# The first transform of the first sequence with x as the loaded operand and its result kept on chip, and a new order of the work

## The chip, the core and the metric

The kernel runs on one core of a Trainium2 chip. TensorE multiplies matrices out of SBUF, the on-chip memory, into PSUM, its accumulation memory; VectorE and ScalarE work element by element and copy results out of PSUM; GpSimd fills a few constants; SyncE issues transfers (DMAs) between DRAM and SBUF. The metric is device time in microseconds (us), the median of several runs. Matmuls name a *loaded* (stationary) operand, whose columns become the rows of the result, and a *streamed* (moving) operand, whose columns become the columns of the result.

## What is computed

For each of 8 sequences of 3200 positions with 256 features:

```python
X = np.fft.rfft(x, axis=1)
Yr = Xr @ w_r - Xi @ w_i + b_r
Yi = Xr @ w_i + Xi @ w_r + b_i
Yr, Yi = shrink(Yr, 0.01), shrink(Yi, 0.01)   # sign(v) * max(|v| - 0.01, 0)
x = np.fft.irfft(Yr + 1j * Yi, n=3200, axis=1)
# then, on that x:
gate = sigmoid(sum over k of conv_w[k] * x delayed by 4 - k positions)
out = (gate * (x @ w_val)) @ w_out
```

All in float32; the moe weights come as 64-bit floats and are turned into 32 bits on chip.

## The kernel before

The transform of length 3200 is done in two steps, 3200 = 50 x 64. A position is n2 * 64 + n1.

1. *p1*, the first step over n2 (50 values): f1, a 50 x 50 matrix of cosines and sines in 64 columns, is the loaded operand and x the streamed one. Two halves h of n1 lie on partitions 0 to 49 and 64 to 113, and two column blocks go to the two halves of the output, so four matmuls of a quarter of the array (50x64) run side by side. The result s is copied to SBUF and stored in DRAM (`a_dram`), eight pieces u per sequence. Function `p1` does this for sequences 1 to 7, `p1_first` for sequence 0, whose x is loaded by SyncE's and ScalarE's queues together.
2. *p2*, 13 steps u of two frequencies t each (the last has one): a load brings the columns of t from `a_dram`, now with (part, n1) on 128 partitions; two fp32 matmuls with the columns as loaded operand and f2 as the streamed one give the spectrum s (line 590). ScalarE and VectorE split it into high and low fp32r parts and a sum of both parts; the products with the weights follow: k_ps (line 665, real plus imaginary with w_r) and y_ps (line 660). Bias, shrinking (lines 671 to 680), and after every second u the first inverse step z_ps (line 703, quarter tiles of 64x64 with g1, which for most t is f2 turned by a product with the identity, line 424). z goes to DRAM (`z_dram`).
3. *positions* and *gated*: z is loaded back (`zl`), the second inverse step y_p (line 759) fills `y_sb`, VectorE runs the taps (line 813), TensorE the two products v_ps and o_ps (line 791, in the last blocks 787), and SyncE stores `out`.

The order of all instructions is worked out when the program is built. Every piece of work is given to `plan.add` with its engine, its due time `at`, its expected length in ns, the pieces it depends on, and the buffer slots it opens. `Plan.order` plays the pieces through: it takes, for each engine, among the pieces that could start first, the one with the smallest due time; a bonus keeps pieces on part tiles (mode `q`) together. Due times are a step number plus an offset from the table `O` (lines 230 to 253). Expected lengths that the prediction uses are those of p1 (890), s2i (950), mix (1404), mix_sum (702) and s1i (1776).

At the start, TensorE has `warm` products on zeros between the four `p1_first` groups (lines 911 to 915). Many loads of constants wait until all 16 stores of sequence 0 have landed (`STORED`), the second part of f2 among them (lines 411 and 922); the weight splits wait until the last p1 group is copied (`START`).

The kernel writes sequence 0's columns and reads them back with these two lines, at the end of `p1_first` and in `p2`:

```python
engines[h][1].dma_start(out=dst[h, :, us[k] * 4 * D:(us[k] + 1) * 4 * D], in_=tl[ks[h]][k * HP:k * HP + N2, :])
nc.sync.dma_start(out=at_[:, 0:n, :], in_=src[:, ts[0]:ts[-1] + 1, :])
```

Of the kernel before, what the change touches and what calls it, by code (L numbers as in the profile page):

```python
# [10 lines left out]
F32 = mybir.dt.float32  # L11
# [21 lines left out]
def dft_constants():  # L33
# [37 lines left out]

    f1b = np.zeros((N2, HP))
    f1b[:, 0:N2] = f1.reshape(N2, N2)
    f2 = f2.reshape(NT, P, 2, N1).transpose(1, 0, 2, 3)
    f2 = np.concatenate([f2[:, :-1].reshape(P, NT // 2, 2, 2, N1).swapaxes(2, 3).reshape(P, -1), f2[:, -1].reshape(P, P)], axis=1)
    out = {"f1": f1b, "f2": f2, "g1": g1[-1].reshape(P, P), "g2": g2.reshape(N2, N2), "eye": np.eye(P)}
# [3 lines left out]
class Plan:  # L80
# [11 lines left out]
    def add(self, at, engine, busy, fn, uses=(), sets=(), new=None, delay=None, mode="r", kb=0, chain=None, extra=0):  # L92
# [10 lines left out]
        p = dict(n=n, at=at, engine=engine, busy=busy, fn=fn, before=before, new=new or {}, mode=mode, kb=kb, extra=extra,  # L103
# [7 lines left out]
    def order(self):  # L111
# [25 lines left out]
        mode, wire = "r", 0.0  # L137
        done = []

# [11 lines left out]
        while len(done) < len(pieces):  # L151
            best = None
            for e in engines:
                could = []
                for p in waiting[e]:
                    at = opens(p)
                    if at is not None:
                        could.append((max(free[e], p["ready"], at, wire - BACKLOG if p["kb"] else 0.0), p))
# [15 lines left out]
            if e == "PE":  # L174
# [3 lines left out]
                busy, delay, mode = busy + to, delay + to, p["mode"]  # L178
            if p["kb"]:
                wire = max(wire, start + 800) + p["kb"] * 1024 / WIRE  # L180
                delay = wire - start + 1400 + p["extra"]
            free[e] = start + busy
# [29 lines left out]
SWITCH = {"rq": 97, "fq": 97, "qr": 100, "qf": 100}  # L212
WEIGHTS = 130
CLOCK = ((40000, 1.6), (45000, 1.15))
WIRE = 230
BACKLOG = 5000
# [6 lines left out]
def act(n, kind="copy"):  # L223
# [7 lines left out]
     'together': 2.272,  # L231
     'later': 4.406,
     'load_x': -3.369,
     'p1': 1.752,
     'p1_step': 1.14,
     'load_a': -3.927,
     's2': -1.558,
     's1i': 1.333,
     'p3': 3.595,
     'load_z': -3.135,  # L240
     'y': 0.522,
     'conv': 1.176,
     'val': 2.74,
     'gate': -3.751,
     'project': 5.91,
     'late_val': 7.079,
     'late_out': 15.503,
     'turn': 0.967,
     'mix_sum': -0.635,
     'p1_1': -0.586,  # L250
     'load_x_1': -0.349,
     'p1_2': -1.603,
     'p3_0': 0.549}
WARM = 2, 1, 1, 1, 10
SLOTS = {"x": 3, "zl": 3, "y_hl": 2, "s1": 2, "a": 3, "xs": 2, "sx": 2, "xz": 1, "yb": 2, "tp": 3, "zst": 2,
# [7 lines left out]
def fourier_filter_then_gated_conv(ctx: ExitStack, tc: tile.TileContext, x, w_r, w_i, b_r, b_i,  # L263
# [5 lines left out]
    dram = ctx.enter_context(tc.tile_pool(name="dram", bufs=2, space=bass.MemoryType.DRAM))  # L269
    LATE_VAL, LATE_OUT = set(LATE[int(O["late_val"]):]), set(LATE[int(O["late_out"]):])  # L270
# [9 lines left out]
    b_sb = const.tile([P, 2 * D + 2 * P], F32, name="b_sb")  # L280
# [704 lines left out]
```

## Time and profile before

| | |
|---|---|
| median of 3 runs | 901.65 us (900.0 to 903.2) |
| profiled execution, span from first to last instruction | 897.1 us |
| TensorE matmul busy | 865.2 us (96%), 10370 records |
| TensorE weight load busy | 741.1 us (83%) |
| VectorE busy | 763.5 us (85%) |
| ScalarE busy | 603.7 us (67%) |
| DMA | 162.26 MB, 181 GB/s on the mean |
| share of the chain that ended last | PE 83%, DVE 10%, DMA 4%, ACT 2% |

The page gives, for one execution, the busy time of each engine and its share in 40 slices (digits are tenths). PE is TensorE, PEld its weight loads, DVE VectorE, ACT ScalarE, POOL GpSimd, SP SyncE; a q behind the name is the engine's instruction queue. A row of a group reads: line, engine, operation, result<-operands, tile of the array where it is a matmul, shape and count | busy us, mean ns of one | idle time of the engine just before and what ended it. An fp32 matmul leaves two records. Rows of the chain read: start, length, what. The profiled execution's own device time is not listed beside its span.

### The profile page before, as it was taken

To read this page: it belongs to the slowest core of one execution; us is meant where nothing else is said; L and a number is where in the kernel's file an instruction comes from. 1 tells how busy PE (TensorE), PEld (TensorE's weight loads), DVE (VectorE), ACT (ScalarE), POOL (GpSimd) and SP (SyncE) were. 2 spreads that over 40 slices of the span, in tenths; PEclk is the share of its full clock that TensorE was granted. 3 is DMA by queue.
4 is the path that set the end of the run, shared out by engine and by line. 5 is a ranking of instruction groups with operands and counts; after the bars stand their busy time and mean duration, and the time that the engine had idled before them with its cause. 6 is when DMAs were issued, how large, how long until landed. Compare 5 with 4: busy or idle time off the path is not lost.

```text
span 897.1 us, 24381 instructions
## 1 busy us (share of the span) xinstructions
PE 865.2 (96%) x10370; PEld 741.1 (83%) x10370; DVE 763.5 (85%) x1139; ACT 603.7 (67%) x924; POOL 4.4 (0%) x11
## 2 busy tenths in 40 slices
PE   7799979999999999999999999999999999999898
PEld 2478758898888988899888988989788899998675
DVE  1267787999899997999789996999969998999896
ACT  1256656877677867777677876877757776875654
POOL 0000000000000000000000000000001000000000
PEclk8889999999999999999999999999999999999999
DMA  6577777635755476555674566645674453513522
GB/s 203 198 233 239 228 227 217 210 130 182 236 180 179 159 229 218 190 183 160 217 235 158 163 204 217 222 131 174 215 223 154 139 172 109 178 62 116 180 75 91
DMA packets 103439, 162.26 MB, mean 181 GB/s; under 512 B 9154, under 2 KB 77636, under 8 KB 103332
## 3 DMA queue, kind: packets, MB, share of 16 engines
q1 hardware_dynamic: 102372, 157.44, 54.8%
q10 hardware_dynamic: 960, 3.28, 1.1%
q8 instruction: 81, 1.33, 0.6%
q14 instruction: 26, 0.21, 0.1%
HBM read 82.04 MB, written 78.64 MB: 179 GB/s over the span
## 4 chain that ended last, share of the span: by engine, by line
PE 83%; DVE 10%; DMA 4%; ACT 2%; issue 1%; ACTq 1%; SPq 0%
PE y_ps L660 14%; PE o_ps L791 13%; PE v_ps L791 12%; PE s L590 10%; PE z_ps L703 9%; PE k_ps L665 8%; PE y_p L759 7%; PE p L543 6%; DVE acc L813 4%; DMA x<-in_x 1%; PE v_ps L787 1%; DVE acc L855 1%; DVE gated L317 1%; DMA f_sb<-in_f 1%; DMA a_dram<-s 1%
## 5 line engine op out<-in xcount | busy, mean ns | idle before, releaser
L813 DVE SCALAR_TENSOR_TENSOR acc<-y_sb,cw_sb,acc 128x800 f32<-128x800 f32 (+1 forms) x264 | 255.9, 1018 | 17.6 <-ACT acc L810 17.2
L660 PE MATMUL y_ps<-w_sb,xs 128*128 128x256 f32 x1152 | 155.4, 284 | 0.6 <-DVE xs L648 0.6
L791 PE MATMUL o_ps<-gated,wo_sb 128*128 128x400 f32 x756 | 155.2, 351 | 0.6 <-DVE acc L855 0.6
L660 PEld LDWEIGHTS y_ps<-w_sb,xs 128*128 128x128 f32 x1152 | 144.5, 189 | 11.3 <-DVE xs L652 3.2
L791 PEld LDWEIGHTS o_ps<-gated,wo_sb 128*128 128x128 f32 x756 | 133.5, 188 | 3.1 <-DVE acc L855 0.8
L791 PE MATMUL v_ps<-y_hl,wv_sb 128*128 128x400 f32 x660 | 131.3, 346 | 0.5 <-ACT o L879 0.5
L590 PE MATMUL s<-f_sb,a 128*128 128x128 f32 x800 | 113.2, 284 | 8.2 <-ACT wo_sb L315 3.4
L791 PEld LDWEIGHTS v_ps<-y_hl,wv_sb 128*128 128x128 f32 x660 | 118.5, 188 | 1.6 <-ACT o L879 0.9
L590 PEld LDWEIGHTS s<-f_sb,a 128*128 128x128 f32 x800 | 101.7, 196 | 20.8 <-issue 6.9
L678 ACT ACTIVATE tp<-yb,nlam 128x512 f32<-128x512 f32 (+1 forms) x104 | 73.7, 708 | 38.7 <-DVE yb L674 38.6
L665 PEld LDWEIGHTS k_ps<-w_sb,xs 128*128 128x128 f32 x576 | 77.2, 190 | 20.8 <-issue 10.5
L703 PE MATMUL z_ps<-tp,g_sb 64*64 64x256 f32 x1536 | 93.4, 381 | 0.0
L665 PE MATMUL k_ps<-w_sb,xs 128*128 128x256 f32 x576 | 91.1, 294 | 1.2 <-DVE yb L671 0.9
L759 PEld LDWEIGHTS y_p<-g_sb,zl 50*64 50x64 f32 x4096 | 68.3, 135 | 18.1 <-issue 7.3
L315 ACT CAST gated<-acc 128x800 fp32r<-128x800 f32 x63 | 54.3, 862 | 38.2 <-DVE acc L855 38.0
L759 PE MATMUL y_p<-g_sb,zl 50*64 50x50 f32 x4096 | 72.5, 219 | 7.1 <-issue 4.2
L680 DVE SCALAR_TENSOR_TENSOR tp<-yb,tp 128x512 f32<-128x512 f32 (+1 forms) x104 | 70.0, 673 | 10.6 <-ACT tp L678 10.5
L671 DVE TENSOR_TENSOR yb<-k_ps,bias_sb 128x512 f32<-128x512 f32 x96 | 65.6, 684 | 15.7 <-PE k_ps L665 15.6
L703 PEld LDWEIGHTS z_ps<-tp,g_sb 64*64 64x64 f32 x1536 | 55.3, 133 | 27.4 <-issue 5.1
L855 DVE TENSOR_TENSOR acc<-v_ps,acc 128x800 f32<-128x800 f32 x64 | 62.9, 984 | 16.1 <-PE v_ps L791 12.7
L674 DVE TENSOR_TENSOR yb<-y_ps,yb 128x512 f32<-128x512 f32 x96 | 65.5, 683 | 7.4 <-PE y_ps L660 6.9
L714 ACT COPY z_t<-z_ps 128x1024 f32<-128x1024 f32 x48 | 48.5, 1010 | 25.7 <-PE z_ps L703 25.1
(80 smaller groups left out, 1016.7 us busy)
## 6 DMA issues: line engine op xcount, KB each, us to landing
zl<-z_dram SPq DMA_DIRECT2D x128, 200.0 KB
out<-o SPq DMA_DIRECT2D x63, 400.0 KB
a<-a_dram SPq DMA_DIRECT2D x96, 256.0 KB
z_dram<-z_t SPq DMA_DIRECT2D x48, 512.0 KB
x<-in_x SPq DMA_DIRECT2D x120, 200.0 KB
a_dram<-s SPq DMA_DIRECT2D x120, 200.0 KB
x<-in_x ACTq DMA_DIRECT2D x8, 200.0 KB
a_dram<-s ACTq DMA_DIRECT2D x8, 200.0 KB
```

The source lines that it names most:

```text
L590: nc.tensor.matmul(spec()[:, c, :, i, :], tl[ka][:, i, c * P:(c + 1) * P], f2_of(i), start=True, stop=True)
L660: nc.tensor.matmul(p[:, 1 - r, :], xm(hx, c, r), w_sb[:, m, hw, c, :], start=k == 0, stop=k == 5)
L665: nc.tensor.matmul(p, sm(hx, c), w_sb[:, 0, hw, c, :], start=k == 0, stop=k == 5)
L671: nc.vector.tensor_tensor(out=buffer(kb, "yb", [P, 2, D]), in0=tl[kk].rearrange("p (a d) -> p a d", a=1).to_broadcast([P, 2, D]), in1=bias ...
L674: add(at + 0.2, "DVE", dve(2 * D), lambda: nc.vector.tensor_tensor(out=yb(), in0=tl[ky], in1=yb(), op=ALU.add), [ky + (0,)], [kb + (0,)])
L678: nc.scalar.activation(out=buffer(kt, "tp", [P, 2, D])[:, 0:n], in_=tl[kb][:, 0:n], func=AF.Relu, bias=nlam)
L680: add(at + 0.2, "DVE", dve(n * D), lambda: nc.vector.scalar_tensor_tensor(out=tl[kt][:, 0:n], in0=tl[kb][:, 0:n], scalar=LAM, in1=tl[kt][: ...
L703: nc.tensor.matmul(p[e * HP:(e + 1) * HP, i, j * D:(j + 1) * D], g[i * HP:(i + 1) * HP, r, e * HP:(e + 1) * HP], tl[kts[j]][i * HP:(i + 1) ...
L759: nc.tensor.matmul(pv[h][e * HP:(e + 1) * HP, c, m, :], zt[half(h), m, c * P + e * HP:c * P + (e + 1) * HP], g2_sb[half(h), :], start=True ...
L791: nc.tensor.matmul(p[:, e, 0:TB], w[:, hw, c, e * P:(e + 1) * P], src(hy, c), start=n == 0, stop=n == 5)
L813: nc.vector.scalar_tensor_tensor(out=acc(c), in0=y_of(c, j), scalar=cw_sb[:, c, j:j + 1], in1=acc(c), op0=ALU.mult, op1=ALU.add)
L855: add(at + O["gate"], "DVE", dve(2 * TB), lambda: nc.vector.tensor_tensor(out=gate(), in0=hn(tl[kv][:, :, 0:TB]), in1=gate(), op=ALU.mult) ...
```

## The change

Sequence 0's first transform. x is loaded in 16 pieces: half r of the features goes to the partition half r, so that each partition holds one n2; 52 rows are read where 50 are used. Each piece is sorted by two copies into `x0`, with n1 inside a feature group. `p1_first` then takes 128 columns of `x0` (two groups of 64 positions n1 for one feature each) as loaded operand and the 50 columns of f1 as streamed one: 64 matmuls per half r, in four groups of 20, 20, 16 and 8. Each group is copied out of PSUM by two copies on ScalarE and two on VectorE, straight to where p2 reads its columns: `a0`, which lies in the memory of `y_sb`. p2 of sequence 0 thus has no load, and nothing of sequence 0 goes through `a_dram`.

The other parts: x of sequences 1 to 7 is loaded with the positions n1 in another order (1 KB pieces), and the rows of f2 and of the identity are permuted to match. Loads of x and z and stores of a move 52 rows instead of 50 (the last x keeps 50), and rows of `a_dram` have a pitch padded by 256 words. The columns of two steps u are loaded at once, by two DMAs, into two slots instead of three. z_ps uses 64x128 tiles, eight matmuls instead of 16 per group; the last z is copied twice. x0 shares its memory with the later y_hl and g_hl; b_sb is gone, its rows go into a zst buffer. f2 comes in parts of 2, 2, 4 and 5 steps, and the first two no longer wait for stores. The zeros ahead of y are filled after z of sequence 0 is stored. The warm-up is 32 products of 64 columns, then 3, 1 and 1 of 256. The bias product is due ahead of the p1 groups, p1 of sequence 1 after step 3 of sequence 0.

The planner gets a model of how instructions are fetched, of eight DMAs in flight and of the cold clock (`CLOCK`, `LANES`, `AHEAD`), new expected transfer sizes, and due times of their own for sequences 0, 1, 6 and 7 in `O`.

```diff
+    def p1_loads():
+        queue = (("SP", nc.sync), ("ACT", nc.scalar))
+        src = x.rearrange("b (n j u) (r c) -> u r (b n) j c", u=NB, j=2 * MB, r=2)
...
+        def load(u, r, q):
+            if r == 0:
+                room(("x", (0, u)), tags[u], 4 * D)
+            dst = tl["x", (0, u)][r * HP:r * HP + NF, :]
+            q.dma_start(out=dst.rearrange("p (j c) -> p j c", j=2 * MB), in_=src[u, r, 0:NF])
+
+        def sort(u, r, h, eng):
+            src = tl["x", (0, u)][half(r), h * 512:(h + 1) * 512].rearrange("p (j q g) -> p q j g", j=MB, q=2)
+            lo = h * NM + MB * u
+            dst = x0[half(r)].rearrange("p (q n g) -> p q n g", q=2, n=N1)[:, :, lo:lo + MB, :]
+            (nc.scalar.copy if eng == "ACT" else nc.vector.tensor_copy)(out=dst, in_=src)
...
+    def p1_first(r, i, at):
+        lo, hi = GROUPS[i]
+        kp = ("p1", (0, r, i))
+        cols = x0[half(r)].rearrange("p (k g) -> p g k", g=64)
+        nb = min(2, (hi - lo) // 4)
+        per = (hi - lo) // nb
         def products():
+            p = two_banks(kp)
+            for g in range(lo, hi):
+                k, s = (g - lo) // per, (g - lo) % per
+                nc.tensor.matmul(p[:, k, s * N2:(s + 1) * N2], cols[:, g], f1_sb[half(r), 0:N2], start=True, stop=True)
+
+        def keep(q, e, eng):
+            src = tl[kp][q * HP:(q + 1) * HP, 0:nb, 0:per * N2].rearrange("p b (g t e) -> p e b g t", g=per, e=2)[:, e]
+            c = r * P + q * 64
+            dst = a0[e * HP:(e + 1) * HP, :, c + lo:c + hi].rearrange("p t (b g) -> p b g t", b=nb)
+            (nc.scalar.copy if eng == "ACT" else nc.vector.tensor_copy)(out=dst, in_=src)
+        n = (hi - lo) * NT
+        add(at, "PE", 110 * (hi - lo), products, [...], [kp + (0,), ("turn", "p1", r, i)], {kp: "ps_2"},
+            mode="q", ins=4 * (hi - lo))
...
         def load():
-            at_ = buffer(ka, "a", [P, 2, D])
-            nc.sync.dma_start(out=at_[:, 0:n, :], in_=src[:, ts[0]:ts[-1] + 1, :])
+            at_ = buffer(ka, "a", [P, 4, D])
+            nt = n if last else 4
+            for e in range(2):
+                src = tl["a_dram", b][4 * u + e:4 * u + 2 * nt:2, 0:NH * NM * D]
+                nc.sync.dma_start(out=at_[e * HP:(e + 1) * HP, 0:nt, :], in_=src.rearrange("t (r c) -> r t c", c=D))
...
+        a_of = lambda i, c: tl[ka][:, odd + i, c * P:(c + 1) * P] if b else a0[:, ts[i], c * P:(c + 1) * P]
...
-                        for e in range(2):
-                            nc.tensor.matmul(p[e * HP:(e + 1) * HP, i, j * D:(j + 1) * D],
-                                             g[i * HP:(i + 1) * HP, r, e * HP:(e + 1) * HP],
-                                             tl[kts[j]][i * HP:(i + 1) * HP, r, :], start=r == 0, stop=r == 1)
+                        nc.tensor.matmul(p[:, i, j * D:(j + 1) * D], g[i * HP:(i + 1) * HP, r, :],
+                                         tl[kts[j]][i * HP:(i + 1) * HP, r, :], start=r == 0, stop=r == 1)
```

More of the change, by code (lines that the diff above doesn't have):

```diff
@@ L90, in __init__, with add @@
         self.opened, self.last = {}, {}
-    def add(self, at, engine, busy, fn, uses=(), sets=(), new=None, delay=None, mode="r", kb=0, chain=None, extra=0):
+    def add(self, at, engine, busy, fn, uses=(), sets=(), new=None, delay=None, mode="r", kb=0, chain=None, extra=0, moves=1, ins=0):
         n = len(self.pieces)
@@ L137, in order, with supplied @@
         mode, wire = "r", 0.0
+        landings = [0.0] * LANES
+        ran, fetched = 0, []
         done = []
+        def supplied(p):
+            m = -(-(ran + p["ins"] - AHEAD) // PACKET)
+            return fetched[m - 1] - p["busy"] * max(0, AHEAD + PACKET * (m - 1) - ran) / p["ins"] if m > 0 and p["ins"] else 0.0
         def opens(p):
@@ L178, in order @@
                 busy, delay, mode = busy + to, delay + to, p["mode"]
+                while PACKET * len(fetched) + TRIGGER <= ran + p["ins"]:
+                    fetched.append(start + p["busy"] * (PACKET * len(fetched) + TRIGGER - ran) / p["ins"] + FETCH)
+                ran += p["ins"]
             if p["kb"]:
@@ new lines, in p1_first @@
+    def p1_first(r, i, at):
[4 more added lines that the diff above has]
+        per = (hi - lo) // nb
+        def products():
+            p = two_banks(kp)
[8 more added lines that the diff above has]
+        n = (hi - lo) * NT
+        add(at, "PE", 110 * (hi - lo), products, [("x0", r, u, h) for u in range(8) for h in range(NH)] + [("f1", 0, 0)], [kp + (0,), ("turn", "p1", r, i)], {kp: "ps_2"},
+            mode="q", ins=4 * (hi - lo))
+        for j in range(4):
+            q, e_ = j // 2, j % 2
+            eng = "DVE" if q != e_ else "ACT"
+            add(at + 0.01 + 0.001 * j, eng, act(n) if eng == "ACT" else dve(n), lambda q=q, e_=e_, eng=eng: keep(q, e_, eng), [kp + (0,)],
+                [("a0", r, i, j)])
@@ L688, in p2 @@
         kts = [("tp", (b, v)) for v in both]
-        gs = [("g1", 2 * v, 0) for v in both]
-        nz = 1 if last else 4
+        gs = [g1_key(v) for v in both]
+        nz = 2 if last else 4
         def s1i():
@@ L743, in load @@
             for h in range(NH):
-                nc.sync.dma_start(out=zt[half(h)], in_=src[h, :, k * MB:(k + 1) * MB, :])
-        add(at + O["load_z"], "SP", 700, load, [("z_dram", b, u) for u in range(NU)], [kz + (0,)], {kz: "zl"}, kb=400, chain="zl")
+                nc.sync.dma_start(out=zt[h * HP:h * HP + NF], in_=src[h, :, k * MB:(k + 1) * MB, :])
+        add(at + off("load_z", b), "SP", 700, load, [("z_dram", b, u) for u in range(NU)], [kz + (0,)], {kz: "zl"}, kb=320, chain="zl", moves=2)
         def views():
@@ L950, in fourier_filter_then_gated_conv @@
                 later_constants(u)
+        if b == 0:
+            add(NU - 0.5, "POOL", 300, lambda: nc.gpsimd.memset(y_sb[:, :, 0, 0:H0 * N2], 0.0),
+                [("z_dram", 0, u) for u in range(NU)], [("y", -1, j) for j in range(3)])
         start = (b + 1) * T + O["p3"] + O.get(f"p3_{b}", 0.0)
```

337 lines of the change are left out of this document (185 added, 152 removed).

## The prediction

> **What bounds the kernel now.** I read the page first: busy shares, then the slices.
>
> ```profile
> span 897.1 us, 24381 instructions
> PE 865.2 (96%) x10370; PEld 741.1 (83%) x10370; DVE 763.5 (85%) x1139; ACT 603.7 (67%) x924; POOL 4.4 (0%) x11
> PE   7799979999999999999999999999999999999898
> DVE  1267787999899997999789996999969998999896
> PEclk8889999999999999999999999999999999999999
> ```
>
> TensorE is busy for 96% of the span, and the slices that fall short are the first two or three and a few at the end. A mean cannot tell what the start costs, so I cut the span into windows (columns: length, then busy time and count for PE, weight load, VectorE, ScalarE and GpSimd, then granted clock, DMA share, GB/s).
>
> ```profile
> 0.00:10.00 10.00, 6.07 (x14) 2.10 (x17) 0.48 (x1) 1.28 (x1) 1.14 (x9) 0.93 0.53 161
> 10.00:20.00 10.00, 9.60 (x46) 2.53 (x39) 2.45 (x2) 2.02 (x2) 0.00 (x0) 0.73 0.76 243
> 30.00:40.00 10.00, 8.01 (x22) 3.53 (x20) 2.12 (x4) 1.16 (x3) 0.00 (x0) 1.00 0.45 160
> 40.00:50.00 10.00, 8.35 (x42) 5.72 (x40) 2.32 (x5) 3.20 (x8) 0.00 (x0) 0.66 0.80 208
> 50.00:60.00 10.00, 10.00 (x87) 8.57 (x80) 7.19 (x14) 6.07 (x12) 0.00 (x0) 1.00 0.83 227
> 100.00:200.00 100.00, 94.55 (x1267) 79.91 (x1266) 89.80 (x166) 68.69 (x111) 0.00 (x0) 0.98 0.64 204
> 800.00:897.00 97.00, 87.82 (x924) 70.20 (x923) 83.26 (x106) 56.82 (x77) 0.00 (x0) 0.99 0.33 111
> ```
>
> From 50 us on, TensorE has no idle time for a long while. Before 50 us it looks busy too, but with 14 to 46 instructions in ten microseconds against 87, and much of that is warm-up filling. Two other stretches leave TensorE idle: 100 to 200 (100 - 94.55 = 5.45 us) and the last 97 us (9.2 us). What the start waits for is told by the chain that ended last:
>
> ```profile
> 29.74 6.81 DMA a_dram<-s
> 36.64 0.39 SPq L574
> 38.41 7.31 DMA f_sb<-in_f
> 45.85 2.05 PE s L590 x8
> 47.90 2.67 PE p L543 x16
> 50.57 0.90 PE k_ps L665 x6
> 51.47 1.40 PE y_ps L660 x12
> ```
>
> The reader should see three things. The last store of the first transform to DRAM takes until 36.6 us. Only then are the columns read back, and a part of the constants f2, held back behind the same stores, lands at 45.7. The first weight product (k_ps) runs at 50.57, and from there the kernel is bound by TensorE. So what the start loses is the time up to 50.57, less the useful work done in it.
>
> **The change, part by part.** *The first transform of sequence 0.* Removed: 64 matmul records of the old products, eight copies of 1024 columns, 16 stores and 13 loads of a, and the wait between them. Added: 16 loads of x by halves of the features, 32 sorting copies into x0, 128 fp32 matmuls of 50 columns with x as the loaded operand, and 32 copies out of PSUM into a0. I follow them in time.
>
> ```profile
> 2.00:4.00 2.00, 2.00 (x3) 0.67 (x2) 0.00 (x0) 0.00 (x0) 0.00 (x0) 1.00 0.60 187
> 42.00:44.00 2.00, 2.00 (x9) 1.37 (x7) 0.00 (x0) 0.96 (x2) 0.00 (x0) 0.66 0.95 230
> x<-in_x ACTq DMA_DIRECT2D x8, 200.0 KB
> ```
>
> Loads: 16 of 52 x 4096 bytes are 3.41 MB, the size of today's. Today's 50-row loads hold the share at 0.60, ten engines of sixteen, 187 / (0.60 x 16) = 19.5 GB/s each. In 42 to 44, with many 1 KB pieces, it is 230 / (0.95 x 16) = 15.1 each. The new pieces are of 512 bytes. I estimate 13 engines for 52 rows, since 10 divides 50 as 13 divides 52; that gives 253 or 197 GB/s and 13.5 or 17.3 us. From a first issue at 1.6 us, with about 1 us to land, the first half is there at 9.4 to 11.3 us and the second at 16 to 20. I take 10.3 and 18.
>
> ```profile
> L671 DVE TENSOR_TENSOR yb<-k_ps,bias_sb 128x512 f32<-128x512 f32 x96 | 65.6, 684 | 15.7 <-PE k_ps L665 15.6
> L647 DVE TENSOR_TENSOR sx<-s,sx 128x256 f32<-128x256 f32 x96 | 39.9, 415 | 24.5 <-ACT xs L644 22.6 <-PE s L590 1.7
> L615 DVE CAST xz<-xs 128x512 fp32r<-128x512 f32 x8 | 3.4, 419 | 0.0
> L453 ACT COPY bias_sb<-bias 128x512 f32<-128x512 f32 x1 | 0.6, 585 | 10.9 <-PE bias L449 10.9
> L317 DVE TENSOR_TENSOR w_sb<-st,w_sb 128x512 fp32r<-128x512 f32 x4 | 2.5, 685 | 0.0
> L341 DVE SCALAR_TENSOR_TENSOR st<-st 128x512 f32<-128x512 f32 x2 | 1.3, 682 | 0.0
> L449 PE MATMUL bias<-b_sb 1*128 1x256 f32 x8 | 2.0, 387 | 0.0
> L451 PE MATMUL bias<-b_sb 1*128 1x256 f32 x4 | 1.2, 408 | 0.0
> ```
>
> Copies: a sort of 512 elements is 0.42 us on VectorE (18 of them, 7.6 us) and 0.585 on ScalarE (14, 8.2 us). The copies out of PSUM have 500, 500, 400 and 200 elements by group, two on each engine, twice over: at 0.68, 0.68, 0.57 and 0.41 on VectorE 4 x 2.34 = 9.4 us. With the weight splits and sums (2.5 and 1.3 us) VectorE has 21 us to do between 4 and 31 us: it fits, without much room. ScalarE has less. So the copies hide behind loads and matmuls, except the last sort (0.59), the last two copies (0.8) and about 1 us by which I let the weight splits push VectorE. If that cover is gone, it is a rival below.
>
> ```profile
> 62.41 0.86 PE p L543 x8
> 66.90 0.89 PE s L590 x8
> 59.82 0.70 PE k_ps L665 x6
> 71.30 1.02 PE p L543 x8
> 60.52 1.89 PE z_ps L703 x32
> 72.31 1.73 PE z_ps L703 x32
> 74.04 0.90 PE k_ps L665 x6
> 788.20 0.92 PE y_p L759 x64
> 120.15 0.43 PE z_ps L695 x2
> ```
>
> Matmuls: no row has a 128-column load in front of a 50-column stream. Lower end: eight records of 128 columns take 0.89 us, so 0.111 each, and two records of 50 columns 2 x 0.043 = 0.087 us. Upper end: a pair never costs more than with 128 columns, 2 x 0.111 = 0.222. I take 0.110, the planner's figure in the diff, because its neighbours agree with the rows (890 against 0.86 us for p, 1404 against 1.40, 702 against 0.70, 950 against 0.92). Half the features are 64 matmuls, 7.0 us. The cold clock (0.73 in 10 to 20 us today) I put at 2.0 us once. First half: 10.3 + 0.6 + 7.0 + 2.0 = 19.9. The second half's x is sorted by 18.6, so TensorE goes on: 26.9. With the last copies 27.7, s2 to 28.6, and the steps up to the sorted sums on ScalarE and VectorE (0.37 + 0.42 + 0.41 + 0.41, and 0.5 between them) put the first k_ps at 30.7 instead of 50.57: 19.9 us earlier. The bias product (2.0 + 1.2 us, today just before 43 us) now stands ahead of the products, where TensorE waits for x. Constants: w_r, w_i, eye and the first 256 KB of f2 follow x on the queue, about 0.85 MB or 4 us after 18, so they land near 22, before 27.7.
>
> Taken back: two p1 of sequence 1 ran before 50.57 and now run later, 2 x 1.02 = 2.0 us; 1 us for VectorE as said. **Start: 19.9 - 2.0 - 1.0 = 17 us gained**, with 0.222 per matmul 14.3 less, with 0.087 up to 3 more. Sequence 1's x loads and stores, moved past the start on SP's queue, have from 22 us until their columns are wanted after thirteen steps, some 60 us; no sequence-0 column traffic competes with them.
>
> *The inverse first step (z_ps).* Eight matmuls of 64x128 replace 16 of 64x64. One full-array matmul of 256 columns takes 0.43; eight of them two at a time give 1.72, and today's group takes 1.73. So nothing is gained in streaming, and half the instructions go. What may be lost is at the boundary. Today z after p takes 1.73, z after another kind 1.89; p after z takes 0.86, p after another kind 1.02. A change between whole and quarter tiles thus costs 0.16, and none is paid between z and p or y_p. Following the chain I find 46 of the 48 groups of z, 15 with p or y_p ahead and 38 with one behind: 53 free boundaries. If half tiles next to quarter tiles pay like whole ones, that is 53 x 0.16 = 8.5 us; if not, nothing. Neither end is nearer, so I take 4.
>
> [...]
>
> *52 instead of 50 rows, padded pitch, a loads in pairs of steps.* All these DMAs run while TensorE is at 10.00 of 10.00, so they are worth nothing in the sum; without that cover it would be 0.2 us for each 200 KB transfer (10 engines against 13 at 19.5 GB/s, 1.05 against 0.83 us). z_t's last copy grows from 256 to 512 elements (some 0.2 us x 8 on ScalarE, 67% busy): nothing.
>
> *The order laid out anew.* TensorE's idle time after 50 us is what an order can win back.
>
> ```profile
> PE s L590 <- ACT wo_sb L315: 3.4, 1, 3.4
> ```
>
> The 5.45 us of 100 to 200 hold one stall of 3.4 us behind the conversion of w_out; the conversion stays, in the same steps. The last 97 us have 9.2. Bounds: 14.6 us won, or about as much lost by worse placing, say 6. I take 2 us won, close to none, since the diff changes none of the work there.
>
> **Sum**: -17 + 4 - 2 = -15 us, span 897.1 - 15 = 882.1. The median of the runs stands 901.65 - 897.1 = 4.55 above this span, so **886.6 us**; its own range is 881 to 890.
>
> **The rivals.** *Every boundary is paid*: +8.5 instead of +4, 891. For: the 0.16 is in the rows wherever tile sizes differ. Against: p to y_p, both with 64-row halves, pays nothing.
>
> *The weight load sets the pace of the new products* (0.222 instead of 0.110): 128 x 0.112 = 14.3 us later, and 886.6 + 14.3 = 901, or 897 without boundaries; call it 900. For: y_p has 64 loads in 0.92 us over four tiles, 57 ns per pair in a tile with a stream of 50 columns that takes 43, so there the load may already bind; twice the columns in a single tile would be 115 per pair. The operand is also read with a step of 64 words. [...]
>
> [...]
>
> *The copies bind instead of DRAM*: if the copies that move between partition halves with steps cost double, VectorE has 2 x 17 + 3.9 = 38 us from 4 us on, and k_ps comes at 44 or so: 13 us of the 17 go, 900. Then the change does not do what it says.
>
> *The order closes the gaps*: most of 14.6 us won, say 9, and no boundary paid: 897.1 - 17 - 9 + 4.55 = 876. For: idle TensorE stands in the windows. Against: the last stretch is bound by VectorE (83.26 of 97 busy).
>
> *Slower: the two half tiles take turns.* Place: z_ps, 48 groups. If tiles with all 128 columns do not run at once, a group costs 8 x 0.43 = 3.44, 48 x 1.71 = 82 us more: 901.65 - 19 + 82 = 965. It decides from 19 / 48 = 0.40 us more per group, that is from 2.13 us. For: no row shows two half tiles at work. Against: quarter tiles run four at once (16 matmuls in 1.73).
>
> **How the numbers follow.** About 0.3%, 2.7 us, is what a measurement of this kernel can tell from none: faster means below 898.9, slower above 904.4. Chances: forecast 0.40, every boundary paid 0.18, load-bound 0.14, copies 0.06, gaps closed 0.16, half tiles in turn 0.06. The two cases at 900 (0.20) split as 0.09 faster, 0.07 same, 0.04 slower. Faster 0.40 + 0.18 + 0.16 + 0.09 = 0.83, same 0.07, slower 0.06 + 0.04 = 0.10. The range runs from 873, a little under the gaps' case, to 900, which leaves out the turns, about half of the cases at 900 and a little below: some 0.18.
>
> **What would show it.** First k_ps near 31 us, no a_dram store before it, and the new products at 0.11 per matmul with 1 us or less between groups; at 0.2 the load binds. VectorE below 9 tenths from 10 to 27 us, else the copies bind. z_ps near 1.73 after p or y_p if boundaries are free, 1.89 if not; over 3 if the tiles take turns. PE records 10370 - 768 - 64 + 256 + 44 = about 9840. TensorE idle after 50 us above 20 us would say the new order lost. The forecast is wrong as a whole if k_ps starts after 40 us, or if steady stretches stretch by more than the boundaries.

## The result, and the profile after

The changed kernel is slower: 956.6 us (median of 4 runs, 955.6 to 959.1) against 902.06 us for the kernel before on the same chip (900.0 to 903.2), a ratio of 1.0625 with a 95% interval of 1.0592 to 1.0657. Ratios here and below compare fast runs alone, so they are not the quotients of the medians beside them. The forecast was 886.6 us, with a range of 873 to 900. The profiled execution has a span of 954.5 us, against 897.1 before.

The page of the changed kernel, busy shares and slices (lines in between left out here):

```profile
span 954.5 us, 23328 instructions
PE 926.2 (97%) x9838; PEld 817.8 (86%) x9838; DVE 775.7 (81%) x1169; ACT 621.0 (65%) x950; POOL 5.5 (1%) x11
PE   9999999999998999999999999999999999999797
DVE  2243669699988899779978998789978999999686
```

TensorE looks fuller than before (97% against 96%, and no thin slice at the start), with 532 records fewer. Busy time alone would call this an improvement. VectorE tells otherwise: its first four slices, some 95 us, are at 2 to 4 tenths, where before the third and fourth were at 6 and 7. What fills TensorE there is told by the chain that ended last (`...` marks rows left out):

```profile
1.46 13.92 PE warm L986 x64
15.37 3.71 PE bias L513 x8
...
20.79 2.86 PE warm L986 x6
23.65 32.38 PE p L590 x152
...
57.17 11.52 PE p L590 x56
...
70.70 10.60 PE p L590 x48
81.30 1.15 PE turned L485 x4
82.45 1.92 PE p L620 x8
84.36 3.71 PE s L673 x16
88.07 1.07 PE p L620 x8
...
89.78 0.71 PE k_ps L748 x6
...
95.34 0.45 PE turned L485 x4
```

The first k_ps starts at 89.78 us instead of 50.57: 39.2 us later, where 19.9 us earlier had been forecast. The 256 records of the new products take 32.38 + 11.52 + 10.60 = 54.5 us, 0.213 each. The 128 products left two records each, so one product costs 0.426 us and not 0.110. From the first k_ps to the end of the span it is 864.7 us, against 846.5 before: another 18.2 us. The two parts add up to the whole difference of the spans, 57.4 us.

Groups of the changed kernel (busy us and mean ns, then idle time before them and what ended it), and the waits between 20 and 90 us (total, times, longest):

```profile
L590 PE MATMUL p<-f_sb,x 50*128 50x50 f32 x256 | 54.7, 416 | 0.0
L590 PEld LDWEIGHTS p<-f_sb,x 50*128 50x128 f32 x256 | 54.2, 307 | 1.5 <-issue 0.9 <-ACT x L567 0.7
L596 ACT COPY y_sb<-p 64x500 f32<-64x500 f32 (+2 forms) x16 | 13.4, 835 | 40.5 <-DVE y_sb L596 22.2 <-PE p L590 18.2
L596 DVE COPY y_sb<-p 64x500 f32<-64x500 f32 (+2 forms) x16 | 13.3, 828 | 44.4 <-ACT y_sb L596 25.9 <-PE p L590 18.5
L785 PE MATMUL z_ps<-tp,g_sb 64*128 64x256 f32 x768 | 97.6, 394 | 2.0 <-ACT s L625 1.9
```

```profile
DVE y_sb L596 <- ACT y_sb L596: 25.9, 10, 7.5
ACT y_sb L596 <- DVE y_sb L596: 22.2, 9, 9.6
```

The weight load is busy for 54.2 of the products' 54.7 us: the load sets the pace. The copies average 0.83 us, and ScalarE and VectorE wait for each other over and over; they run one after the other, though they are meant to share the work. The page gives no granted clock below full speed for this start because its first clock record comes only at 88.2 us. The durations give it: eight records of the bias product take 3.71 us at 15.37, where run 3 below has them in 1.92 at full clock; 16 records of s take 3.71 us at 84 us, 0.232 each, where the row of before had 0.89 for eight, 0.111 each; four records of `turned` take 1.15 us at 81.3 and 0.45 at 95.3. TensorE stood at half speed through the whole first transform. The fourth execution of the changed kernel, which took no longer, confirms it: its mean granted clock is 0.959 over 955.1 us, against 0.989 to 0.993 in the other three, and that is some 78 us at half speed (2 x 0.041 x 955.1, an estimate).

One window of the changed kernel (columns as in the prediction) shows the load of x:

```profile
10.00:20.00 10.00, 10.00 (x37) 8.94 (x37) 3.37 (x9) 2.02 (x4) 0.00 (x0) 1.00 0.97 161
```

The DMA engines are taken for 0.97, where I had estimated 13 of 16 (0.81), and move 161 GB/s, 10.4 GB/s per engine; I had put 15.1 to 19.5 on these pieces of 512 bytes.

### The profile page after: what moved, and what is told of

It reads as the page before. It is cut to its first block, busy times and chain, and to the rows that moved or that the text cites. A ratio compares the mean times of both kernels' runs of the same rounds, so it can differ in the third digit from the quotient of the medians.

```text
span 954.5 us, 23328 instructions
## 1 busy us (share of the span) xinstructions
PE 926.2 (97%) x9838; PEld 817.8 (86%) x9838; DVE 775.7 (81%) x1169; ACT 621.0 (65%) x950; POOL 5.5 (1%) x11
## 4 chain that ended last, share of the span: by engine, by line
PE 75%; DVE 17%; ACT 4%; DMA 2%; issue 1%; SPq 0%; ACTq 0%; DVEq 0%
PE y_ps L743 11%; PE o_ps L872 11%; PE v_ps L872 10%; PE z_ps L785 8%; PE s L673 8%; DVE acc L894 7%; PE k_ps L748 6%; PE p L590 6%; PE y_p L840 5%; PE p L620 5%; PE warm L986 2%; DVE share L378 2%; DVE acc L936 2%; DMA a_dram<-s 1%; DVE xs L731 1%
## 5 line engine op out<-in xcount | busy, mean ns | idle before, releaser
L894 DVE SCALAR_TENSOR_TENSOR acc<-y_sb,cw_sb,acc 128x800 f32<-128x800 f32 (+1 forms) x264 | 257.9, 1021 | 15.8 <-ACT acc L891 15.4
L872 PE MATMUL o_ps<-share,wo_sb 128*128 128x400 f32 x756 | 156.6, 352 | 1.0 <-ACT y_sb L847 0.7
L872 PEld LDWEIGHTS o_ps<-share,wo_sb 128*128 128x128 f32 x756 | 134.0, 189 | 6.6 <-ACT acc L891 1.6
L872 PE MATMUL v_ps<-share,wv_sb 128*128 128x400 f32 x660 | 131.0, 346 | 0.0
L872 PEld LDWEIGHTS v_ps<-share,wv_sb 128*128 128x128 f32 x660 | 119.4, 188 | 2.0 <-issue 1.0
L673 PE MATMUL s<-f_sb,a 128*128 128x128 f32 x700 | 100.2, 282 | 6.0 <-ACT acc L905 2.6
L673 PEld LDWEIGHTS s<-f_sb,a 128*128 128x128 f32 x700 | 88.8, 192 | 19.4 <-issue 10.1
L785 PE MATMUL z_ps<-tp,g_sb 64*128 64x256 f32 x768 | 97.6, 394 | 2.0 <-ACT s L625 1.9
L376 ACT CAST share<-acc 128x800 fp32r<-128x800 f32 x63 | 54.4, 863 | 54.7 <-DVE acc L936 53.3
L748 PEld LDWEIGHTS k_ps<-w_sb,xs 128*128 128x128 f32 x576 | 76.4, 188 | 14.4 <-issue 10.1
L785 PEld LDWEIGHTS z_ps<-tp,g_sb 64*128 64x128 f32 x768 | 71.2, 189 | 19.8 <-issue 3.7
L960 ACT COPY o<-o_ps 128x800 f32<-128x800 f32 x63 | 51.8, 822 | 28.6 <-PE o_ps L872 28.1
```

Source lines behind the costliest of these rows:

```text
L673: nc.tensor.matmul(spec()[:, c, :, i, :], a_of(i, c), f2_of(i), start=True, stop=True)
L748: nc.tensor.matmul(p, sm(hx, c), w_sb[:, 0, hw, c, :], start=k == 0, stop=k == 5)
L785: nc.tensor.matmul(p[:, i, j * D:(j + 1) * D], g[i * HP:(i + 1) * HP, r, :], tl[kts[j]][i * HP:(i + 1) * HP, r, :], start=r == 0, stop=r == 1)
L872: nc.tensor.matmul(p[:, e, 0:TB], w[:, hw, c, e * P:(e + 1) * P], src(hy, c), start=n == 0, stop=n == 5)
L894: nc.vector.scalar_tensor_tensor(out=acc(c), in0=y_of(c, j), scalar=cw_sb[:, c, j:j + 1], in1=acc(c), op0=ALU.mult, op1=ALU.add)
```

## The experiments

**Clock, stride and the inverse step.** The first four kernels each change one part. Run 1 takes z_ps back to quarter tiles, run 2 puts half tiles into the kernel before, run 3 makes the filling (`warm`, products on zeros) wide again. Run 4 sends sequence 0 through DRAM like the other sequences, also with wide filling; it does not bring the old start back, since x of sequence 0 then comes by SyncE's queue alone, where the kernel before used two queues.

```diff
 # 1: after, z_ps as before (2: the reverse of it, in before)
-    nc.tensor.matmul(p[:, i, j * D:(j + 1) * D], g[i * HP:(i + 1) * HP, r, :], ...)
+    for e in range(2):
+        nc.tensor.matmul(p[e * HP:(e + 1) * HP, i, j * D:(j + 1) * D], g[i * HP:(i + 1) * HP, r, e * HP:(e + 1) * HP], ...)
 # 3: after, filling of 512 columns instead of 64 and 256
+WARM_RUN = ((14, 512),), ((6, 512),), ((1, 512),), ((1, 512),)
 # 4: after, sequence 0 with the code of the others, filling of 512 columns
-    for h in range(NH):
-        for i in range(len(GROUPS)):
-            p1_first(h, i, -40 + 10 * h + i)
+    for u in range(8):
+        p1(0, u, -40 + u)
```

> The changed kernel, but z_ps again as 16 matmuls of 64x64 tiles per group, in the same order of work. If every boundary between half and quarter tiles is paid (z after p or y_p 1.93 us in the changed kernel against 1.73 before, y_p after z 1.08 against 0.92, p after z 1.02 against 0.86): z at 1.73 and 1.89 again, y_p and p after z at 0.92 and 0.86, and about 8 to 10 us less, 947 us. If the longer times come from the new order and not from the tile size: within 2 us of 956.6.

> The kernel before, with z_ps alone as 8 matmuls of 64x128 tiles per group. If boundaries are paid: 53 free boundaries of 0.16 us become dear and each group takes 0.04 more, 53 x 0.16 + 48 x 0.04 = 10 us, 912 us. If half the instructions help and boundaries are free: 900 to 902. If the half tiles took turns: over 960.

> The changed kernel with warm-up products of 512 columns (14, 6, 1 and 1 of them) in the places of the 64- and 256-column ones, same order. Theory: TensorE ran at half clock until 87 us because the short streams never raised the clock, and a 128-column fp32 load takes 0.213 us per record at half clock and 0.107 at full clock. Then a full clock is granted within the first 10 us and the 256 product records take 27 us instead of 54.5, if the clock stays: first k_ps near 50 us, total near 917; if the load-bound products let it fall again, something between 925 and 950. Rival, the strided loaded operand or the load itself takes 0.213 at any clock: products stay at 0.213 per record, total within 10 us of 956.6.

> The changed kernel with sequence 0 sent through the same p1, store and load as the other sequences, and wide warm-up products; half-tile z_ps, order table and everything else as in the changed kernel. Theory: the start alone costs 39 us, so first k_ps near 50 us and a total near 917. Rival, the new order or the new transfers lose the time after the start: total above 930 with k_ps near 50.

Run 1 measured 950.5 us (ratio 1.059, 1.0559 to 1.0622), run 2 906.3 against 904.35 (1.0068, 1.0019 to 1.0117), with a span of 901.6. So the half tiles cost some 3 us by the ratios of run 1 and of the changed kernel, whose intervals overlap, and 6 by run 2, whose interval allows 1.7 to 10.6; the spans give 4.0 and 4.5. That is a tenth of the loss or less. What they change is seen where z_ps stands between two groups of p, before and then in run 2:

```profile
90.09 1.02 PE p L543 x8
91.11 1.73 PE z_ps L703 x32
92.84 0.86 PE p L543 x8
```

```profile
89.49 1.02 PE p L543 x8
90.50 1.93 PE z_ps L702 x16
92.43 1.02 PE p L543 x8
```

Run 3 measured 962.3 us (1.0718, 1.0685 to 1.075), no gain at all. Two of its windows, with the granted clock as third figure from the end:

```profile
25.20:28.20 3.00, 3.00 (x15) 3.00 (x15) 0.00 (x0) 0.00 (x0) 0.00 (x0) 1.00 0.89 272
32.00:35.00 3.00, 3.00 (x16) 3.00 (x15) 0.92 (x2) 0.00 (x0) 0.00 (x0) 0.50 0.40 84
```

At full clock 15 product records fit into 3 us, at half clock 16. My first theory after the result, that the half clock makes the products slow, falls: something takes about 0.21 us per record at any clock. And the clock, full after the wide filling, fell some 3 us after the first product (1.00 granted from 25.2 to 28.2 us, 0.50 from 30 us on) although TensorE issued without a pause. The traces of before and after give the granted clock in records of 3.41 us or whole multiples of it; the expectations call that a window.

Run 4 gave 941.1 us (1.0493), a number of neither theory. Without the new transform the first k_ps came at 70.0 us and the rest was 873 us. So the DRAM route, too, is 20 us later here than it was before; which of the changes to it does that, no run separates.

**The step of 64 words.** Run 5 (on run 3) lays x0 out so that the 128 columns of a load lie side by side. Run 6 streams 128 columns per load instead of 50, the transform's 64-column matrix twice. Run 7 adds quarter tiles and drops five of the second block's six fillings, run 8 takes the due times of the kernel before (all but one entry, for f2).

```diff
 # 5
-    dst = x0[half(r)].rearrange("p (q n g) -> p q n g", ...)
+    dst = x0[half(r)].rearrange("p (g q n) -> p q n g", ...)
-    cols = x0[half(r)].rearrange("p (k g) -> p g k", g=64)
+    cols = x0[half(r)].rearrange("p (g k) -> p g k", g=64)
 # 6, where the bank has room
+    wide = f1_sb[half(r), :].rearrange("p (a n) -> p a n", a=1).to_broadcast([N2, 2, HP])
 # 7, on top of 6: WARM_RUN ((14, 512),), ((1, 512),), ...; z_ps in quarter tiles
 # 8, on top of 7: the table O of the kernel before
```

> As e3_wide_warm (wide warm-up products), but the sorting copies write x0 so that the 128 columns of one product lie next to each other instead of 64 words apart; same instructions otherwise. In e3 the product records stood 0.217 us apart both at full clock (25.1 to 28.4 us) and at half clock. Theory: the step of 64 words in the loaded operand sets 0.217 at any clock. Then records stand 0.107 to 0.111 apart while the full clock is granted, as those of line 590 do in the kernel before, and 0.213 when it falls to half; if it falls after one window of 3.4 us as in e3, the first k_ps moves by less than 10 us, total 950 to 962. Rival, a 128-column load before a 50-column stream takes 0.217 whatever the layout: no change of the pace at full clock.

> As e5_contiguous_load, and each product streams 128 columns (f1's 64 columns twice) instead of 50, all but the last two of ten in a PSUM bank; the surplus columns are overwritten by the next product. Theory: the clock falls because a 50-column stream leaves the array idle for most of each load, so with streams as long as the loads the full clock stays granted, all 256 records at 0.107 to 0.113, 28 us instead of 54.5, first k_ps near 62 us and a total near 932. Rival, the clock follows the rows of the array or something else: it falls to half about 3.4 us after the products begin and the products take over 45 us.

> As e6_contiguous_wide_stream, with one wide warm-up product instead of six ahead of the products and z_ps on quarter tiles again. If the three costs add (7 us of warm-up, 6 us of z_ps as e1 and e2 showed, the products at 0.11): first k_ps near 55 us, total near 919. What is then left above the kernel before (902 to 904) is the new order after the start, some 12 us, and 4 us at the start.

> As e7_both_mended, with the table of due times of the kernel before (no entries of their own for sequences 0, 6 and 7, except one for f2). If the new due times lose time after the start (from first k_ps to the end 861 us in e1 against 846.5 before): 8 to 12 us less than e7, near 909. If the loss comes from the transfers or from chance: within 3 us of e7.

Run 5: 957.95 us (1.063, 1.0531 to 1.073). The same two windows as for run 3:

```profile
25.20:28.20 3.00, 3.00 (x28) 3.00 (x28) 0.00 (x0) 0.00 (x0) 0.00 (x0) 1.00 0.89 275
32.00:35.00 3.00, 3.00 (x16) 3.00 (x16) 2.04 (x3) 2.95 (x4) 0.00 (x0) 0.50 0.46 94
```

Now the clock shows: 28 records in 3 us at full speed (0.11 each), 16 at half. So there are two limits of the same size. A load with a step of 64 words takes 0.21 us at full clock, and a contiguous one takes 0.21 at half clock. Either alone keeps the slow pace, which is why mending one of them moved the time so little.

Run 6 (958.9 us, 1.0641) kept the pace of run 5, 20 records at half clock in 4.27 us (0.214), with more than twice the stream, so the load sets the pace and not the stream; its clock fell all the same (16 wide records took 1.85 us at 28.42 us and 3.55 at 30.77). Run 7 (952.2, 1.0561) had half the clock from the first products on: its first 16 records, at 21.05 us, took 3.78 us, against 1.98 in run 6. Run 8 (965.5, 1.0704) is 13 us slower than run 7: the new due times by themselves are not what loses the time. Runs 5, 6 and 10 rest on two executions each.

**Two row halves at once.** The two halves of the features use 50 rows each, in different halves of the array. Run 9 issues them alternately, in seven groups of up to ten columns, bias first, with contiguous loads, 10 wide fillings and quarter tiles. Run 10 is run 9 with one half after the other in each group.

```diff
 # 9
+    for g in range(lo, hi):
+        for r in range(2):
+            nc.tensor.matmul(p[:, r, s * N2:(s + 1) * N2], cols[half(r), g], f1_sb[half(r), 0:N2], ...)
 # 10
-    for g in range(lo, hi):
-        for r in range(2):
+    for r in range(2):
+        for g in range(lo, hi):
```

> Same result as the changed kernel, contiguous columns and quarter-tile z_ps as in e7, but the products of both halves of the features alternate, one on rows 0 to 49 and one on rows 64 to 113 of the array, in seven groups of ten columns for both halves, each half with its own PSUM bank; the planner is given 214 ns per pair; 50-column streams; the bias product stands ahead of wide warm-up products that last until x is there. Theory: in e5 to e7 the full clock was lost one window after the products began, with 50- and with 128-column streams alike, because only 50 of 128 rows were at work; with both row halves loaded and streamed at once the full clock stays granted, a pair of matmuls takes 0.21 to 0.23 us, all of them 14 to 16 us, first k_ps 40 to 43 us instead of 88, total 903 to 910 if the loss after the start stays at 15 us. Rival, the clock follows the streamed columns per load: it falls to half, pairs take 0.43, 27 us, k_ps near 55, total near 920. Rival, the two halves do not overlap: 27 us at full clock and 54 at half.

> As e9_paired_rows, with the same tiles, copies and order, but in each group the ten products of the first half of the features stand before the ten of the second, so that one row half works at a time. Theory: 0.213 us per matmul at full clock while it lasts, and the clock falls to half within two windows (3.4 to 6.8 us) of the first product, then 0.427: about 50 us of products and k_ps some 33 us later than in e9. Rival, pairing is not what matters: same pace and clock as e9.

Run 9 is the best version found, 930.2 us (1.0314, 1.026 to 1.0369), and still slower than before; run 10 measured 951.4 (1.0553, 1.0491 to 1.0614). Chain of run 9, then of run 10:

```profile
26.44 8.77 PE p L590 x78
...
37.22 8.71 PE p L590 x80
...
47.08 8.71 PE p L590 x80
```

```profile
25.73 11.41 PE p L590 x60
...
39.15 14.79 PE p L590 x80
...
55.09 14.79 PE p L590 x80
```

Eighty records take 8.71 us side by side and 14.79 in turn (0.185 each, where one half alone had 0.213; why it is less, no run shows). The first k_ps comes at 68.6 and 83.5 us. All of it is at half clock: run 9's TensorE had waited 5.1 us for x, up to 26.44 us, and the clock fell in that wait (1.00 granted from 20 to 25 us, 0.53 from 25 to 30).

**Keeping the clock.** Run 11 is run 9 with 17 instead of 10 fillings, so that TensorE does not wait for x. Run 12 adds the 128-column stream. Runs 13 and 14 (with wide and narrow streams) split each copy by rows of the result, run 15 by accumulator bank, run 16 by bank and with separate places to write to.

```diff
 # 11
-WARM = ((10, 512),), ((1, 512),)
+WARM = ((17, 512),), ((1, 512),)
 # 13, 14: eight copies of half the rows instead of four
+    ts_ = slice(0, NT // 2) if eng == "ACT" else slice(NT // 2, NT)
 # 15, 16: eight copies, one bank each
+    r = 0 if eng == "ACT" else 1
 # 16: a0 as two pieces, one for each r
+    a0 = y_sb.rearrange("p c h n -> p (c h n)")[:, 0:NT * D].rearrange("p (r t c) -> p r t c", c=P, r=2)
```

> The paired-rows kernel with a longer warm-up: 17 instead of 10 matmuls of 512 columns stand ahead of the first transform, so that TensorE is busy until about 27.5 us and does not wait 5.1 us for the input of sequence 0 (20.9 to 26.4 us there). Theory A, the clock fell in that wait and only work on all rows brings it back, while products on 2 x 50 of 128 rows can hold it: the granted clock stays near 1.00 through the products, a pair of matmuls takes about 0.22 us instead of 0.43, the 64 pairs and what lies between them (27.4 and 4.9 us there) end by about 46 us, k_ps starts at 50 to 55 us and the time is 930 - 15 = 915 us. Theory B, products of this kind do not hold the clock whatever goes ahead of them: it falls to 0.50 within some 8 us of the first product, as with contiguous columns and one half at a time, k_ps starts at 66 to 70 us and the time is 927 to 932 us.

> The same (longer warm-up, paired rows), and each product streams 128 columns instead of 50: the 64 columns that hold the 50 of the transform, twice, where the bank has room (8 of 10 products of a group); the surplus is overwritten by the product after it or not read. Theory A (rows hold the clock): as the run beside it, about 915 us, since 128 columns of stream took 0.111 us per record at full clock before, no more than the load. Theory C, the clock follows how many row-columns are streamed in a stretch, so 100 rows alone are too little with 50 columns, and enough with 128: the run beside it falls to 0.50 and this one stays near 1.00, k_ps at 50 to 55 us, about 915 us against about 930. Theory B (products do not hold it in any form): both fall, both 927 to 932 us.

> The paired-rows kernel with long warm-up and 128-column streams, and each copy out of the accumulators split in two parts: ScalarE copies the first 12 of the 25 rows, VectorE the other 13, so that what they write is apart and neither waits for the other. Theory A (the copies' turns made TensorE wait, 4.1 us a group against 2.35 us of products at full clock, and the wait took the clock): ScalarE and VectorE run side by side, about 2.2 us a group, the seven groups end by about 45 us, the clock stays at 1.00 or near it, k_ps starts at 48 to 53 us instead of 63.2, and the time is 915 to 925 us instead of 935.6. Rival (products of this kind lose the clock without any wait): the clock falls by 36 us although TensorE waits nowhere over 0.3 us, records take 0.107 a piece (0.43 a pair of matmuls) from there, k_ps is at 60 us or later and the time is 930 us or more.

> The same with streams of 50 columns. If only waiting takes the clock: as the run beside it, k_ps at 48 to 53 us, 915 to 925 us. If the amount of work streamed counts too (at 50 columns the array is streamed through for less than half of the loads' time): the clock falls by 40 us and stays at half until the next transform's work, k_ps at 57 to 62 us, 925 to 935 us, while the run beside it keeps the clock.

> The kernel of the split copies with 128-column streams, split another way: ScalarE copies the accumulator bank of the first half of the input columns, VectorE the bank of the second half; the rows that they write to interleave. Theory A (they took turns because both read one bank): both engines copy at the same time, 4 x 0.6 = 2.4 us a group, TensorE waits little, the clock holds beyond 40 us, k_ps at 48 to 55 us, 915 to 925 us. Theory B (they take turns because of where they write): still one after the other, k_ps at 63 to 69 us, 935 to 940 us.

> The same, and the copied columns are laid out so that what ScalarE writes lies in one piece and what VectorE writes in another. Theories A and B both say side by side here: 2.4 us a group, the clock holds if only waiting takes it, k_ps at 48 to 55 us, 915 to 925 us. If the engines still take turns, both fall; if they don't and the clock falls all the same with no wait over 0.3 us on TensorE, the products themselves lose the clock: k_ps at 57 to 62 us and 925 to 935 us.

Measured: 937.95 us for run 11 (1.0419), 935.6 for run 12 (1.0409), 939.1 (1.0416), 939.4 (1.0434), 939.4 (1.0431) and 939.25 (1.0419) for runs 13 to 16; their intervals all lie between 1.033 and 1.0495. None came near 925. Runs 11 and 12 have their first k_ps at 64.7 and about 63 us, earlier than run 9 with 68.6, and lose more than that after it (873 and 868 us from there to the end, against 858.5). By the clock records TensorE is at half speed for 11 us of that stretch in run 9, 32 in run 11 and 21 in run 12. Windows and TensorE's timeline of run 11:

```profile
27.20:31.60 4.40, 4.40 (x80) 4.40 (x80) 3.98 (x6) 2.25 (x3) 0.00 (x0) 1.00 0.93 186
37.00:41.00 4.00, 4.00 (x38) 4.00 (x40) 2.01 (x2) 1.65 (x2) 0.00 (x0) 0.50 0.00 0
```

```profile
27.08 4.67 PE L590 MATMUL p<-f_sb,x 50*128 50x50 f32 x80
...
33.86 2.74 PE L590 MATMUL p<-f_sb,x 50*128 50x50 f32 x40 [1.06 <-DVE y_sb L595]
36.98 4.51 PE L590 MATMUL p<-f_sb,x 50*128 50x50 f32 x40 [0.38 <-DVE y_sb L595]
```

With the clock kept and the rows paired, 80 records take 4.4 us, 0.055 each, so a product costs 0.11 us: the figure of my forecast, reached only with all three mended. Then the copies bind. TensorE waits for them 1.06 us, the clock falls some 2 us later (1.00 granted from 30 to 35 us, 0.58 from 35 to 40), and the products after that run at half speed. The copies' part of the timeline of run 16 (ScalarE, then VectorE), where the two engines read different banks and write apart:

```profile
32.82 0.57 ACT L600 COPY y_sb<-p 64x250 f32<-64x250 f32 x1 [0.64 <-DVE y_sb L600]
33.42 0.58 DVE L600 COPY y_sb<-p 64x250 f32<-64x250 f32 x1 [0.64 <-ACT y_sb L600]
```

They still take turns, 0.6 us each. So neither a shared bank nor interleaved rows is the reason by itself, and theories A and B of run 15 both fall. The trace says what does it: each copy starts 0.03 us after the other engine's ends, and the profile puts the end of its wait down to a semaphore of that copy. The order stands in the program: as built from run 16's `kernel.py`, each of these copies but the first of a group waits for a semaphore that the copy before it, on the other engine, raises. Built with VectorE's copies writing to another tile, the program keeps these waits; built with an accumulator tile for each half, it has none. So the shared accumulator tile brings them; no run shows what separate tiles would gain. In all six runs the clock fell during such a wait (1.1 to 3.2 us) or within 2 us of its end, with narrow and wide streams alike. That the wait takes it is likely by this, but not shown: unpaired products lost it without a wait in runs 3, 5 and 6, and no run kept paired ones going long enough without one. In runs 12 and 16 it came back for some 6.8 us from wide paired products on (0.78 and 0.90 granted from 45 to 50 and 50 to 55 us in run 12, 0.68 and 1.00 from 40 to 45 and 45 to 50 us in run 16) and in run 6 during wide unpaired ones (48 records in 7.44 us at 70.40 us, where 48 at 39.31 us took 9.68), in runs 13 and 15 it didn't (0.50 granted from 40 to 60 us): what raises it isn't settled.

## Why the prediction was wrong

**What bounds the kernel now** was read rightly in the main: the time to the first k_ps weighs most, and most of the loss lies there (39.2 of 57.4 us).

**The price of a product, 0.110 us, is the step that failed.** The forecast named a lower end of 0.087 and an upper end of 0.222 and took the figure in the diff, since its neighbours agreed with rows of the trace. No row backed this one. It measured 0.426, nearly twice the upper end, because that end came from rows at full clock with contiguous loads, and neither holds here. For 128 products it is 128 x 0.316 = 40.4 us. The rival "the weight load sets the pace" had the right mechanism (the load is busy for 54.2 of 54.7 us) and the right suspicion, the step of 64 words; its price was half of the true one, as it charged neither for the step nor for half speed, and each alone doubles it: at full clock run 3 has 15 records in 3 us with the step and run 5 has 28 without, two records in 0.21 us, the rival's 0.222. "The cold clock, 2.0 us once" was a second wrong term: the clock stayed at half speed to the end of the transform. With the step in place that cost the products nothing more, as run 3 shows, but it did cost the filling, the bias product and the groups in between.

**The rest of the start** was mis-sized too, in smaller terms. The first product was put at 10.9 us (10.3 and a sort of 0.6) and started at 23.65: 12.8 us late. VectorE had sorted its part of the first half by 13.6 us, so the load accounts for some 3 us of that (it takes some 21 us in all, 3.41 MB at 161 GB/s, and not 13.5 to 17.3). The rest went to work that TensorE had ahead of the products, at half speed: the last two copies of that half stood on ScalarE behind the copy of the bias, which could start only at 19.12 us, and behind them came another filling, to 23.65. The products with what lies between them were put at 16.0 us and took 58.8 (23.65 to 82.45), from there to k_ps 3.8 and took 7.3. The three differences, 12.8 + 42.8 + 3.5, are the 59.1 us between 30.7 and 89.78. The 2.0 us "taken back" for two p1 of sequence 1 were not due: these run ahead of the first k_ps here too (82.45 and 88.07 in the chain) and take 3.0 of the 7.3 us.

**The copies**: 0.68 us was forecast for 500 elements on VectorE, with the two engines side by side. They took 1.0 us on either engine (1.00 to 1.03 in runs 9 and 11) and went in turns, so the four copies of a group need 4.1 us. The rival "the copies bind" put them at double, 1.36, too dear for one copy and too cheap for two in turn; in the changed kernel the slow products hide them, and they bind in runs 11 to 16, where the products are fast.

**z_ps**: a border between half and quarter tiles is paid: between groups of p, run 2 has z_ps at 1.93 us where 1.73 stood before, and p after it at 1.02 where 0.86 stood; after a whole tile z_ps takes 1.93 against 1.89. In the time it is 3 to 6 us by runs 1 and 2; I had taken 4, with 8.5 as the end. That the two half tiles take turns did not happen (1.93 is far from 3.44); that the measured time lies near the 965 of that rival is chance.

**The order, -2 us**, has the wrong sign. Windows of the kernel before, then of the one after, from the first k_ps to 60 us before the end and from there:

```profile
50.57:837.00 786.43, 772.08 (x9707) 683.60 (x9709) 704.44 (x1066) 557.98 (x862) 3.28 (x2) 1.00 0.58 185
837.00:897.00 60.00, 53.65 (x536) 40.65 (x528) 47.61 (x57) 34.04 (x46) 0.00 (x0) 0.99 0.32 109
```

```profile
89.78:894.00 804.22, 788.81 (x8977) 701.38 (x8975) 702.99 (x1068) 560.37 (x864) 4.77 (x3) 1.00 0.62 183
894.00:954.50 60.50, 49.05 (x492) 35.05 (x484) 46.55 (x56) 30.58 (x41) 0.00 (x0) 0.94 0.27 90
```

TensorE's idle time is 15.4 + 11.5 us after and 14.4 + 6.4 before, 6.2 more, most of it in the last 60 us, where the clock also falls to 0.94. (The forecast's bound of 14.6 us for what an order can win left out the windows that it had not cut: it is 20.7.) TensorE is busy 837.86 - 825.72 = 12.1 us longer. z_ps itself holds some 4 of that, 97.6 us after in the row shown above and in the row of before

```profile
L703 PE MATMUL z_ps<-tp,g_sb 64*64 64x256 f32 x1536 | 93.4, 381 | 0.0
```

93.4 us. But what follows z_ps pays for the border too. Run 2, the kernel before with the half tiles and nothing else, in the same two stretches:

```profile
49.39:841.60 792.21, 781.70 (x8954) 695.72 (x8955) 705.15 (x1066) 561.63 (x864) 3.29 (x2) 1.00 0.57 184
841.60:901.60 60.00, 53.42 (x508) 40.85 (x507) 47.79 (x57) 32.99 (x44) 0.00 (x0) 0.97 0.30 104
```

It is busy 835.1 us, 9.4 more than before, and idle 17.1, 3.6 less, so that 5.8 us reach the time. If busy time at half clock counts as half of itself, by the clock records of the traces, TensorE's work from the first k_ps on is some 822 us before, 831 in run 2, 833 in the changed kernel, and 823 to 826 in every run of it with quarter tiles (1 and 7 to 16). By this estimate the 18.2 us are some 8 of half tiles, 2 of other work, 2 of half clock (13.7 us of it, against 7.9) and 6 of waiting.

**Why the waits and the falls of the clock grow is open.** Taking the half tiles back won less than 8 us, since waits and half clock grew further there: run 1 is idle for 28 us of this stretch and at half clock for 19. With the due times of before it got worse (run 8), so the table by itself is not the cause. The rest is 858 to 873 us in runs 9 to 16, with quarter tiles, and 873 in run 4, without the new transform, so it does not hang on the first transform's form.

**52 rows, padded pitch** at nothing: no run tests it by itself. **The count of records**, about 9840, was 9838. By the forecast's own test, a first k_ps after 40 us, it was wrong as a whole. The rivals were wrong with it: none of them let the start lose time, since the new products were priced throughout with rows at full clock and contiguous loads.

## What to carry to other kernels

When a change swaps which operand is loaded, price the load from a row of the same shape, step and clock; a planner's figure is no row, even if its neighbours agree. Where a slow pace has two causes of equal size, mending one shows nothing, so look at the pace in a window where the other is known to be absent. And follow a stage that is made of thin matmuls to the next two limits, its copies out (two engines that share an accumulator tile were put in turn by the program) and the clock (in runs 11 to 16 it fell from 1.00 to 0.50 during a wait of 1.1 to 3.2 us for them or within 2 us of its end), before calling it shorter than a trip through DRAM.

## What the runs showed of the hardware

- A 128-column float32 load took 0.11 us contiguous and 0.21 us with a step of 64 words at full clock (28 and 15 records in 3 us, runs 5 and 3), and 0.21 either way at half clock (0.213 with the step in the changed kernel, 0.214 contiguous in run 6).
- A change between tiles of 64x128 and 64x64 cost 0.16 to 0.2 us each time (p after z_ps 1.02 against 0.86, z_ps after p 1.93 against 1.73, run 2 against before).
- TensorE issuing without a pause did not suffice for the full clock: in the changed kernel 54.5 us of products on 50 rows, with 50 columns each, stayed at half speed (0.213 per record), and in runs 3, 5 and 6 the clock fell from 1.00 to 0.50 within 3 to 5 us of the first product, with no wait. With filling of 128 rows and 512 columns ahead of them it was full: run 3 has 28 records of it in 13.90 us, 0.50 each, and two in 2.00 us later at half clock.
- Two products on different halves of the rows overlap almost fully: 80 records in 4.4 us at full clock, 0.055 each (run 11), against 0.11 with one half at a time (run 5).
- A copy of 64 x 500 float32 elements out of the accumulators, with steps, took 1.00 us on ScalarE and on VectorE alike, and one of 250 elements 0.57 to 0.6 (runs 9 and 16).
